# Attention and MLP on one core: a 128-wide left slice, normalisation in pieces, a fixed engine order

## The chip, the core and the metric

The kernel runs on one core of one Trainium2 chip. The metric is device time in microseconds (us) of one execution. The kernel before took 793.80, 796.29 and 796.85 us in three runs (median 796.29).

## What is computed

Eight batches, 12 heads, 448 tokens, head width 64. q and k are normalised per token and head, attention follows without a mask, the heads are joined to x of 768 columns, and a LayerNorm with an MLP of 3072 hidden columns is added to x. In numpy, cut:

```
q_n, k_n = rmsnorm(q, g_q), rmsnorm(k, g_k)
attn = softmax(q_n @ k_n.T / 8)
x = heads_joined(attn @ v)                # [8, 448, 768]
xn = (x - mean) / sqrt(var + 1e-6) * g_ln
out = x + relu(xn @ w_ch1) @ w_ch2
```

## The kernel before

Class `_Fast` does the work (lines 47 to 429). A last check on the softmax sums (`flag`, L408) would send the data through `_general`; the two are joined at L583 to L585.

**Attention** goes by head pairs: 6 pairs a batch, 48 in all. The 448 tokens of a head are 384, of which a partition holds three, and 64 left over; the left tokens of a pair's two heads share one group of 128 partitions. A unit is two pairs: `load_unit` (L89) brings q, k and v with three main loads and six for the leftovers on the SP queue, into one of two buffers. `prep_unit` (L102) normalises: Square on ScalarE (L108), sums on VectorE (L109), the root (`_rsqrt`, L31: a first guess by ScalarE's Exp from the exponent, then three Newton rounds on VectorE), k times g_q·g_k (L119) and times its root (L121), k as a high and a low half-precision part (L123, L124), q (L125, L127); v is cast on GpSimd (L129, L132). `trans_k` (L137) and `trans_q` (L151) turn seven groups each on TensorE, and VectorE copies the result to SBUF.

A pair has seven steps i. `scores(p, i)` (L164) multiplies 128 keys with 448 queries and ScalarE takes the exponential (L180); i = 6 has the leftover keys of both heads. `values(p - 1, i)` (L183) multiplies the pair before with v: three slices of 128 queries go to the accumulator oA (L202), the last 64 queries to oB (L204). A ones column in v gives the softmax sum, and `evac_o` (L208) divides by it.

**LayerNorm** (`ln`, L279 to L300) takes statistics of whole token tiles (three of 128 per batch, four in odd batches, whose fourth holds the leftovers of two batches), its root, and normalises on VectorE (L298). `ln_trans` (L302) turns it on TensorE. **The MLP** comes as chunks of six matmuls (`mlp_chunks`, L312): 24 `up` chunks (L323, Relu on ScalarE L325), then eight `down` chunks per tile (L334, added to x on VectorE L338, stored by SP, L353).

**The order.** `attention` (L226) is a generator; `run` (L359) draws steps from it with `upto`. It draws pair 0, then 12 loads of W1 between the next pairs (`load_w1`, L257: SP loads 256 columns into one of two staging buffers, GpSimd multiplies six times by g_ln, L264), then W2 by a casting load on GpSimd's queue (L268), then up to pair 7. After that, while batch b's MLP chunks are emitted, the steps of the next six pairs are drawn between them so that they are through at 0.78 of the chunks; then `ln` of the next batch, whose transposes go between the last chunks. The framework's scheduler orders each engine's instructions from this program; each engine and each DMA queue then runs its own in order.

Of the kernel before, what the change touches and what calls it, by code (L numbers as in the profile page):

```python
# [10 lines left out]
INT32 = mybir.dt.int32  # L11
# [6 lines left out]
LN2 = 0.6931471805599453  # L18
# [5 lines left out]
NU = 3  # L24
UH = H // NU
UG = UH * 3 + UH // 2
EXP_BIAS = -4.0
REC_LO, REC_HI = 1.0 / 3.0e7, 0.5


def _rsqrt(nc, eng, out, a, t0, t1, iters=3):  # L31
    eng.tensor_copy(out=t0, in_=a.bitcast(INT32))
    eng.tensor_scalar(out=t0, in0=t0, scalar1=2.0 ** -23, scalar2=-127.0,
                      op0=ALU.mult, op1=ALU.add)
    nc.scalar.activation(out, t0, AFT.Exp, scale=-0.5 * LN2)
    for _ in range(iters):
        eng.tensor_tensor(out=t1, in0=out, in1=out, op=ALU.mult)
        eng.tensor_tensor(out=t1, in0=t1, in1=a, op=ALU.mult)
        eng.tensor_scalar(out=t1, in0=t1, scalar1=-0.5, scalar2=1.5, op0=ALU.mult, op1=ALU.add)
        eng.tensor_tensor(out=out, in0=out, in1=t1, op=ALU.mult)  # L40
# [6 lines left out]
class _Fast:  # L47


    def __init__(self, ctx, tc, sh, q, k, v, w1, w2, out):  # L50
# [5 lines left out]
        self.p_t = pool("p_t", 1)  # L56
# [6 lines left out]
        self.p_st = pool("p_st", 2)  # L63
# [7 lines left out]
        self.v16 = [fix.tile([128, UH, 3, D + 1], FP16, name=f"v{i}", tag=f"v{i}") for i in range(3)]  # L71
        self.vl = [fix.tile([128, UH // 2, 2, D + 1], FP16, name=f"vl{i}", tag=f"vl{i}")
                   for i in range(3)]
        for t in self.kT:
            nc.vector.memset(t[:, 1], 0.0)
        for t in self.v16:
            nc.vector.memset(t[:, :, :, D], 1.0)
        for t in self.vl:
            nc.vector.memset(t, 0.0)
            nc.vector.memset(t[0:64, :, 0, D], 1.0)  # L80
            nc.vector.memset(t[64:128, :, 1, D], 1.0)
        self.rec = fix.tile([128, B * NPAIR, 3, 2], FP32, name="rec_all", tag="rec_all")
# [6 lines left out]
    def load_unit(self, u):  # L89
        nc = self.nc  # L90
        b, hs = u // NU, (u % NU) * UH
        t = self.p_in.tile([128, 3, UG, D], FP32, tag="qkv")
        for n, src in enumerate((self.q, self.k, self.v)):
            nc.sync.dma_start(
                t[:, n, 0:UH * 3].rearrange("p (h j) d -> p h (j d)", j=3),
                src[b, hs:hs + UH, 0:384].rearrange("h (p j) d -> p h (j d)", j=3))
            left = src[b, hs:hs + UH, 384:448].rearrange("(g e) p d -> e p g d", e=2)
# [4 lines left out]
    def prep_unit(self, u):  # L102
        nc, sh = self.nc, self.sh
        t = self.loads.pop(u)
        ssq = self.p_n.tile([128, 2, UG], FP32, tag="ssq")
        for n in range(2):
            sq = self.p_t.tile([128, UG, D], FP32, tag="sq", name="sq")
            nc.scalar.activation(sq, t[:, n], AFT.Square)  # L108
            nc.vector.tensor_reduce(out=ssq[:, n], in_=sq, axis=AX.X, op=ALU.add)  # L109
        msq = self.p_n.tile([128, 2, UG], FP32, tag="msq")  # L110
        nc.vector.tensor_scalar(out=msq, in0=ssq, scalar1=1.0 / D, scalar2=1e-6,
                                op0=ALU.mult, op1=ALU.add)
        rr = self.p_n.tile([128, 2, UG], FP32, tag="rr")
        t0 = self.p_n.tile([128, 2, UG], FP32, tag="rt0")
        t1 = self.p_n.tile([128, 2, UG], FP32, tag="rt1")
        _rsqrt(nc, nc.vector, rr, msq, t0, t1)
        qn = self.p_n.tile([128, UG, 2, D], FP16, tag="qn")
        khl = self.p_n.tile([128, UG, 2, D], FP16, tag="khl")
        nc.vector.tensor_tensor(out=t[:, 1], in0=t[:, 1],  # L119
                                in1=sh.gprod.unsqueeze(1).broadcast_to([128, UG, D]), op=ALU.mult)  # L120
        nc.vector.tensor_tensor(out=t[:, 1], in0=t[:, 1],  # L121
                                in1=rr[:, 1].unsqueeze(2).broadcast_to([128, UG, D]), op=ALU.mult)
        nc.vector.tensor_copy(out=khl[:, :, 0], in_=t[:, 1])  # L123
        nc.vector.tensor_tensor(out=khl[:, :, 1], in0=t[:, 1], in1=khl[:, :, 0], op=ALU.subtract)  # L124
        nc.vector.tensor_tensor(out=qn[:, :, 0], in0=t[:, 0],  # L125
                                in1=rr[:, 0].unsqueeze(2).broadcast_to([128, UG, D]), op=ALU.mult)
        nc.vector.tensor_copy(out=qn[:, :, 1], in_=qn[:, :, 0])  # L127
        v16, vl = self.v16[u % 3], self.vl[u % 3]
        nc.gpsimd.tensor_copy(out=v16[:, :, :, 0:D],  # L129
                              in_=t[:, 2, 0:UH * 3].rearrange("p (h j) d -> p h j d", j=3))  # L130
        for e in range(2):
            nc.gpsimd.tensor_copy(out=vl[64 * e:64 * e + 64, :, e, 0:D],  # L132
                                  in_=t[64 * e:64 * e + 64, 2, UH * 3:UG])
        self.units[u] = (qn, khl, v16, vl)


    def trans_k(self, p):  # L137
        nc, sh = self.nc, self.sh
        qn, khl, v16, vl = self.units[p // 2]
        w = p % 2  # L140
        ps = self.ps_tr.tile([128, 1024], FP16, tag="tr")
        kT = self.kT[p % 2]
        gs = [UH * 3 + w] + [6 * w + i for i in range(6)]
        for i, g in enumerate(gs):
            nc.tensor.matmul(ps[:, ts(i, 128)], khl[:, g], sh.id16, is_transpose=True,  # L145
                             start=(i == 0), stop=(i == 6))
        flat = kT.rearrange("p g d -> p (g d)")
        nc.vector.tensor_copy(out=flat[:, 0:64], in_=ps[:, 0:64])  # L148
        nc.vector.tensor_copy(out=flat[:, 128:960], in_=ps[:, 64:896])  # L149

    def trans_q(self, p):  # L151
        nc, sh = self.nc, self.sh
        qn, khl, v16, vl = self.units[p // 2]
        w = p % 2
        ps = self.ps_tr.tile([128, 1024], FP16, tag="tr")
        qT = self.p_qT.tile([128, 896], FP16, tag="qT")
        gs = [6 * w, 6 * w + 1, 6 * w + 2, UH * 3 + w, 6 * w + 3, 6 * w + 4, 6 * w + 5]
# [3 lines left out]
        nc.vector.tensor_copy(out=qT, in_=ps[:, 0:896])  # L161
        self.prs[p] = dict(qT=qT, kT=self.kT[p % 2])

    def scores(self, p, i):  # L164
# [6 lines left out]
        ps = self.ps_s.tile([128, 512], FP32, tag="psS")  # L171
# [11 lines left out]
    def values(self, p, i):  # L183
        nc = self.nc
        c = self.prs[p]
        qn, khl, v16, vl = self.units[p // 2]
        w = p % 2
        E = c["E"]
        if i == 0:
            c["oA"] = self.ps_o.tile([128, 3, 130], FP32, tag="oA", name="oA")  # L190
            c["oB"] = self.ps_o.tile([64, 130], FP32, tag="oB", name="oB")
        oA, oB = c["oA"], c["oB"]
        if i < 6:
            h, j = divmod(i, 3)
            rhs = v16[:, 2 * w + h, j]
            cs = slice(65 * h, 65 * h + 65)
            m0, l0 = (0, 384) if h == 0 else (64, 0)
        else:
            rhs = vl[:, w].rearrange("p e d -> p (e d)")
            cs, m0, l0 = slice(0, 130), 0, 384  # L200
        for t in range(3):
            nc.tensor.matmul(oA[:, t, cs], E[:, i, m0 + 128 * t:m0 + 128 * t + 128], rhs,  # L202
                             start=(i == 0 and t == 0), stop=(i == 6 and t == 2))
        nc.tensor.matmul(oB[:, cs], E[:, i, l0:l0 + 64], rhs, start=(i == 0), stop=(i == 6))  # L204
# [3 lines left out]
    def evac_o(self, p):  # L208
        nc = self.nc
# [5 lines left out]
        rec, recl = self.rec[:, p], self.recl[:, p]  # L215
        nc.vector.reciprocal(rec, oA[:, :, :, D])
        nc.vector.reciprocal(recl, oB[:, :, D])
        nc.vector.tensor_tensor(  # L218
            out=x[:, :, 128 * hp:128 * hp + 128].rearrange("p t (e d) -> p t e d", e=2),
            in0=oA[:, :, :, 0:D], in1=rec.unsqueeze(3).broadcast_to([128, 3, 2, D]), op=ALU.mult)  # L220
# [3 lines left out]
            in0=oB[:, :, 0:D], in1=recl.unsqueeze(2).broadcast_to([64, 2, D]), op=ALU.mult)  # L224

    def attention(self):  # L226

        n = B * NPAIR
        self.load_unit(0)
        self.load_unit(1)  # L230
        self.prep_unit(0)
        self.trans_k(0)
        self.trans_q(0)
        for p in range(n + 1):
# [5 lines left out]
            if p % 2 == 0 and p // 2 + 1 < B * NU:  # L240
                if p // 2 + 2 < B * NU:
                    self.load_unit(p // 2 + 2)
                self.prep_unit(p // 2 + 1)
            for i in range(7):
                if p < n:
                    self.scores(p, i)
                    yield p + (i + 0.5) / 7
                if p > 0:
                    self.values(p - 1, i)
                    yield p + (i + 1) / 7  # L250
                if p + 1 < n and i == 2:
                    self.trans_k(p + 1)
                if p + 1 < n and i == 4:
                    self.trans_q(p + 1)


    def load_w1(self, c0, c1):  # L257

        nc, sh = self.nc, self.sh
        st = self.p_st.tile([128, NDC, 256], FP32, tag="st", name="st")  # L260
        nc.sync.dma_start(st[:, :, 0:c1 - c0],
# [354 lines left out]
```

## Time and profile before

| | |
|---|---|
| median of three runs | 796.29 us |
| the profiled execution | 795.19 us, its span 793.4 us |
| TensorE (PE) busy | 697.7 us, 88% of the span, 5114 matmuls |
| VectorE (DVE) busy | 455.2 us, 57%, 1229 instructions |
| ScalarE (ACT) busy | 322.0 us, 41%, 609 instructions |
| GpSimd (POOL) busy | 119.8 us, 15%, 154 instructions |
| mean granted TensorE clock | 0.97 of 2.4 GHz |
| HBM read, written | 51.97 MB, 11.01 MB |

Times in the rows are microseconds from the span's start unless ns is said. PEld is TensorE's weight load, which overlaps PE. A row of the chain of waits gives start, duration and what it was, on the path that ended last. A group's row gives line, engine, operation, output and inputs with shapes, count, then busy time, mean ns of one, and idle time before them with what ended it. Matmuls are pipelined, so a busy TensorE need not be at its peak.

### The profile page before, as it was taken

The numbers are of one execution on the slowest core, as the hardware profiler recorded it, in microseconds if no ns is written. First come the engines' busy times: TensorE is split into PE (matmuls) and PEld (weight loads), VectorE is DVE, ScalarE is ACT, GpSimd is POOL, SyncE is SP. The second block draws the span as 40 slices with busy tenths as digits, with TensorE's granted clock in tenths as the row PEclk, the third lists the DMA queues.
The fourth block names the chain that finished last, engine by engine and source line by source line (L and its number), as shares of the span: only waits on it lengthen the run. The fifth ranks groups of instructions, "written<-read, shape, count | busy, mean of one in ns | idle before, by whom it ended". The sixth has DMA issues, their size and how long they took to land. (4 is left out here: it accounts for less than half of the span.)

```text
span 793.4 us, 12901 instructions
## 1 busy us (share of the span) xinstructions
PE 697.7 (88%) x5114; PEld 419.7 (53%) x5114; DVE 455.2 (57%) x1229; ACT 322.0 (41%) x609; POOL 119.8 (15%) x154
## 2 busy tenths in 40 slices
PE   0276438999999989999999999998999999999996
PEld 0144225655555656656555556655555666664453
DVE  2949369888546783678545683677545452334011
ACT  2163434743364316643464226642464216512400
POOL 2579992000000000010000000010000000000000
PEclk9997777999999999999999999999999999999999
DMA  8993642523021130233022130233020110001011
GB/s 195 239 259 124 190 131 70 140 71 110 21 71 46 61 95 21 70 91 91 21 71 64 47 97 14 70 91 90 21 70 1 40 41 1 2 21 41 0 41 43
DMA packets 76531, 59.17 MB, mean 75 GB/s; under 512 B 23728, under 2 KB 72880, under 8 KB 76464
## 3 DMA queue, kind: packets, MB, share of 16 engines
q1 hardware_dynamic: 72256, 53.49, 22.8%
q0 software_dynamic: 3136, 4.72, 3.3%
q8 instruction: 42, 0.69, 0.4%
q10 hardware_dynamic: 1072, 0.07, 0.1%
q14 instruction: 25, 0.20, 0.1%
HBM read 51.97 MB, written 11.01 MB: 79 GB/s over the span
## 5 line engine op out<-in xcount | busy, mean ns | idle before, releaser
L334 PE MATMUL psC<-w,hT 128*128 128x384 f16 x1344 | 245.8, 329 | 0.0
L323 PE MATMUL psH<-xnT,w 128*128 128x512 f16 (+1 forms) x1152 | 243.3, 353 | 1.8 <-DVE xnT L310 1.8
L180 ACT ACTIVATE E<-ps 128x448 f16<-128x448 f32 x336 | 178.3, 541 | 127.7 <-PE ps L174 100.5
L325 ACT ACTIVATE hT<-psH 128x384 f16<-128x384 f32 (+1 forms) x192 | 104.2, 543 | 162.6 <-PE psH L323 162.6
L334 PEld LDWEIGHTS <-hT 128*128 128x128 f16 x1344 | 125.8, 98 | 77.7 <-issue 1.9
L323 PEld LDWEIGHTS <-w 128*128 128x128 f16 x1152 | 106.5, 98 | 92.2 <-issue 2.6
L174 PE MATMUL ps<-qT,kT 128*128 128x448 f16 x288 | 105.7, 374 | 12.3 <-ACT E L180 7.6
L202 PEld LDWEIGHTS <-E 128*128 128x128 f16 x1008 | 72.7, 100 | 76.2 <-ACT E L180 16.9
L129 POOL CAST v<-t 128x768 f16<-128x768 f32 x24 | 22.0, 917 | 488.8 <-issue 430.5
L202 PE MATMUL oA<-v,E 128*128 128x65 f16 x864 | 74.5, 197 | 16.7 <-ACT E L180 10.4
L109 DVE TENSOR_REDUCE ssq<-sq 128x14 f32<-128x896 f32 x48 | 52.0, 1083 | 64.2 <-ACT sq L108 64.2
L108 ACT ACTIVATE sq<-t 128x896 f32<-128x896 f32 x48 | 45.5, 949 | 80.9 <-DMA t<-in_q_dram 66.0
L264 POOL TENSOR_SCALAR w<-st,gln 128x256 f16<-128x256 f32 x72 | 77.0, 1086 | 9.2 <-DMA st<-in_moe_w_ch_dram 8.9
L338 DVE TENSOR_TENSOR x<-psC,x 128x384 f32<-128x384 f32 x48 | 26.3, 548 | 80.9 <-PE psC L334 80.7
L145 PE MATMUL ps<-id,khl 128*128 128x128 f16 x336 | 29.9, 235 | 38.1 <-DVE khl L124 38.1
L204 PE MATMUL oB<-v,E 128*64 128x65 f16 x288 | 61.5, 219 | 0.4 <-DVE xl L222 0.4
L161 DVE COPY qT<-ps 128x896 f16<-128x896 f16 x48 | 29.7, 619 | 37.7 <-PE ps L159 37.5
L148 DVE COPY kT<-ps 128x64 f16<-128x64 f16 x48 | 9.0, 187 | 69.9 <-PE ps L145 69.7
L204 PEld LDWEIGHTS <-E 128*64 128x64 f16 x336 | 35.3, 107 | 25.3 <-issue 4.3
L145 PEld LDWEIGHTS <-khl 128*128 128x128 f16 x336 | 23.4, 106 | 44.7 <-DVE khl L124 38.4
L174 PEld LDWEIGHTS <-kT 128*128 128x128 f16 x288 | 27.9, 99 | 17.0 <-issue 5.3
L159 PE MATMUL ps<-id,qn 128*128 128x128 f16 x336 | 28.6, 228 | 5.1 <-DVE kT L149 4.9
(71 smaller groups left out, 549.7 us busy)
## 6 DMA issues: line engine op xcount, KB each, us to landing
t<-in_q_dram SPq DMA_DIRECT2D x24, 384.0 KB, 3.5
t<-in_k_dram SPq DMA_DIRECT2D x24, 384.0 KB, 4.3
t<-in_v_dram SPq DMA_DIRECT2D x24, 384.0 KB, 4.4
st<-in_moe_w_ch_dram SPq DMA_DIRECT2D x12, 768.0 KB, 5.1
out_dram<-x SPq DMA_DIRECT2D x24, 384.0 KB, 2.3
w<-in_moe_w_ch_dram POOLq DMA_DIRECT2D x4, 1152.0 KB, 13.4
t<-in_q_dram SPq DMA_DIRECT2D x48, 32.0 KB, 3.7
t<-in_k_dram SPq DMA_DIRECT2D x48, 32.0 KB, 3.8
```

The lines of the kernel that those rows point to most:

```text
L108: nc.scalar.activation(sq, t[:, n], AFT.Square)
L109: nc.vector.tensor_reduce(out=ssq[:, n], in_=sq, axis=AX.X, op=ALU.add)
L145: nc.tensor.matmul(ps[:, ts(i, 128)], khl[:, g], sh.id16, is_transpose=True, start=(i == 0), stop=(i == 6))
L161: nc.vector.tensor_copy(out=qT, in_=ps[:, 0:896])
L174: nc.tensor.matmul(ps[:, 0:S], kT[:, 192 + 128 * i:320 + 128 * i], qT[:, h * S:(h + 1) * S], start=True, stop=True)
L180: nc.scalar.activation(out=c["E"][:, i], in_=ps[:, 0:S], func=AFT.Exp, scale=1.0 / 8.0, bias=EXP_BIAS)
L202: nc.tensor.matmul(oA[:, t, cs], E[:, i, m0 + 128 * t:m0 + 128 * t + 128], rhs, start=(i == 0 and t == 0), stop=(i == 6 and t == 2))
L204: nc.tensor.matmul(oB[:, cs], E[:, i, l0:l0 + 64], rhs, start=(i == 0), stop=(i == 6))
L264: nc.gpsimd.tensor_scalar(out=sh.w1[:, dc, c0:c1], in0=st[:, dc, 0:c1 - c0], scalar1=sh.gln[:, dc:dc + 1], scalar2=None, op0=ALU.mult)
L323: nc.tensor.matmul(ps[:, 0:N], sh.w1[:, dc, ts(f, 128)], xnT[:, dc, 0:N], start=(dc == 0), stop=(dc == NDC - 1))
L325: nc.scalar.activation(out=hT[:, f, 0:N], in_=ps[:, 0:N], func=AFT.Relu)
L334: nc.tensor.matmul(ps[:, 0:384], hT[:, f, ts(t, 128)], sh.w2[:, f, ts(g, 384)], start=(f == 0), stop=(f == NFF - 1))
```

## The change

- The value matmul for the last 64 queries takes the 128 queries 320 to 447 as weights; rows 64 to 127 of its output are used. qT puts each head's 64 left queries last, so all slices start at multiples of 128, and the last score step has two matmuls of 448 columns in place of three.
- Units of batch 0 are one pair, and their buffers lie in hT, which the MLP uses later; units of the other batches stay two pairs. Their preparation is a list of 11 pieces, spread over the steps before the pair that needs them; a unit's loads are issued when the unit two ahead of it is prepared.
- k times g_q·g_k goes to GpSimd. The root has two rounds, and takes its guess from the integer bits in one Exp.
- W1 comes by three casting loads on GpSimd's queue, without g_ln; W2 by two.
- LN statistics are taken per pair (128 columns). LN's root, its passes (now ScalarE's Identity with scale and bias, then VectorE's product with g_ln) and its transposes are pieces between the last chunks, from 0.82 of a batch's MLP on.
- The first value matmuls of a pair are drawn one step later.
- TensorE, ScalarE, GpSimd and SP run in program order (`manual_schedule`); VectorE's order is still the scheduler's.

```diff
 def _rsqrt(nc, out, a, t, eps):
+    eng.tensor_scalar(out=a, in0=a, scalar1=eps, scalar2=None, op0=ALU.add)
+    nc.scalar.activation(out, a.bitcast(INT32), AFT.Exp, scale=-0.5 * LN2 * 2.0 ** -23,
+                         bias=0.5 * LN2 * (127.0 - 0.043))
+    for _ in range(2):
+        eng.tensor_tensor(out=t, in0=out, in1=out, op=ALU.mult)
+        eng.scalar_tensor_tensor(out=t, in0=t, scalar=-0.5, in1=a, op0=ALU.mult, op1=ALU.mult)
+        eng.scalar_tensor_tensor(out=out, in0=t, scalar=1.5, in1=out, op0=ALU.add, op1=ALU.mult)
...
 def load_unit(self, u):
+        if m == 1:
+            o = 2688 * (u % 3)
+            t = self.hT.rearrange("p f n -> p (f n)")[:, o:o + 2688].bitcast(FP32)
...
+        eng = nc.scalar if u < 2 else nc.sync
+        for n, src in ((1, self.k), (0, self.q), (2, self.v)):
...
-                nc.sync.dma_start(t[64 * e:64 * e + 64, n, UH * 3:UG], left[e])
+                eng.dma_start(t[64 * e:64 * e + 64, n, mh * 3:g], left[e])
...
 def prep_ops(self, u):
+        return [lambda: (begin(), square(1), kg()), lambda: total(1), lambda: square(0),
+                lambda: (total(0), vmain()), root, None, kn, khi, klo, qn, qdup, vleft]
...
 def scores(self, p, i):
-            nc.tensor.matmul(ps[:, 0:384], kT[:, 64:192], qT[:, 512:896], start=False, stop=False)
-            nc.tensor.matmul(ps[:, 384:448], kT[:, 64:192], qT[:, 448:512], start=False, stop=True)
+            nc.tensor.matmul(ps[:, 0:S], kT[:, 64:192], qT[:, S:2 * S], start=False, stop=True)
...
 def values(self, p, i):
-            c["oB"] = self.ps_o.tile([64, 130], FP32, tag="oB", name="oB")
+            c["oB"] = self.ps_o.tile([128, 130], FP32, tag="oB", name="oB")
...
-        nc.tensor.matmul(oB[:, cs], E[:, i, l0:l0 + 64], rhs, start=(i == 0), stop=(i == 6))
+        nc.tensor.matmul(oB[:, cs], E[:, i, 320:448], rhs, start=(i == 0), stop=(i == 6))
...
 def attention(self):
+        for u in range(1, nu):
+            p, m = UNIT_PAIR[u], UNITS[u][2]
+            st, e = max(7 * (p - 1 - m) + 2, last + 1), 7 * (p - 1) + 1
+            last = e
+            ops = self.prep_ops(u)
+            for x, op in enumerate(ops):
+                if op is not None:
+                    todo.setdefault(max(0, st + (e - st) * x // (len(ops) - 1)), []).append(op)
+            if u + 2 < nu and u + 2 > 2:
+                todo.setdefault(max(0, e), []).append(lambda u=u: self.load_unit(u + 2))
+        for u in range(3):
+            self.load_unit(u)
...
+                    for x in {0: (), 1: (0, 1)}.get(i, (i,)):
+                        self.values(p - 1, x)
+                if p > 1 and i == 1 and (p - 1) % NPAIR:
+                    self.stats(p - 2)
...
 def load_w1(self, c0, c1):
-        nc.sync.dma_start(st[:, :, 0:c1 - c0],
...
+        self.nc.gpsimd.dma_start(
+            out=self.sh.w1[:, :, c0:c1],
...
 def ln_ops(self, b):
+        def norm(t):
...
+            nc.scalar.activation(out=t32, in_=tiles[t], func=AFT.Identity,
+                                 scale=c["rs"][:, t:t + 1], bias=c["sh"][:, t:t + 1])
+            nc.vector.tensor_tensor(out=c["xn", t], in0=t32, in1=sh.gln, op=ALU.mult)
+
+        res = [root, lambda: norm(0)]
+        for t in range(1, n):
+            res += [lambda t=t: norm(t), lambda t=t: self.ln_trans(c["xn", t - 1], t - 1)]
+        return res + [lambda: self.ln_trans(c["xn", n - 1], n - 1)]
...
 def run(self):
+        upto(0.4)
+        for c in range(0, FF, 1024):
+            self.load_w1(c, c + 1024)
+        upto(3)
+        for n0 in range(0, NFF, 12):
+            self.load_w2(n0, n0 + 12)
         upto(7)
...
+        for op in self.ln_ops(0):
+            op()
+            upto(self.pos + 0.1)
+        frac = 0.82
...
+                upto(min(goal, start + (goal - start) * done / total / frac))
+                if self.pos >= goal:
+                    if items is None:
+                        items, at, left = self.ln_ops(b + 1), 0, len(chunks) - 1 - i
+                        per = len(items) / max(left - 1, 1)
+                        due = 0.0
+                    due += per
+                    while at < len(items) and at + 1 <= due + 1e-6:
+                        items[at]()
+                        at += 1
...
+        with tc.manual_schedule(engines={ENG.PE, ENG.Activation, ENG.Pool, ENG.SP}):
+            _Fast(fctx, tc, sh, q, k, v, moe_g_ln, moe_w_ch1, moe_w_ch2, out).run()
```

## Rows read from the trace of the kernel before

**Rows 1.** Stretches: us, busy of PE, PEld, DVE, ACT, POOL (count), clock, DMA, GB/s

```profile
0.00:131.40 131.40, 58.84 (x492) 37.41 (x493) 85.25 (x234) 46.56 (x85) 92.62 (x103) 0.86 0.71 182
131.40:205.00 73.60, 70.39 (x528) 43.69 (x528) 65.21 (x179) 35.45 (x71) 3.10 (x6) 1.00 0.30 87
```

**Rows 2.** One line, L323: ns min/median/max, first and last start, forms

```profile
L323 PE MATMUL psH<-xnT,w x1152: 322/358/390, 131.4 to 754.9; 128*128 128x384 f16 x96, 128*128 128x512 f16 x96
```

**Rows 3.** The chain of waits from 655 to 662 us

```profile
656.03 0.50 PE ps L159 x7
656.52 0.19 PE ps L174
656.71 0.09 PE oA L202 x3
656.80 0.15 PE oB L204
656.95 1.08 PE psH L323 x6
```

**Rows 4.** The chain of waits of the whole span

```profile
594.62 0.29 PE ps L174
...
648.20 0.97 PE psH L323 x6
```

**Rows 5.** Waits before 131.4 us: total, times, longest

```profile
ACT sq L108 <- DMA t<-in_q_dram: 32.8, 4, 10.4
```

**Rows 6.** Waits of SP's queue before 131.4 us

```profile
SPq L261 <- POOL w L264: 39.6, 7, 8.1
```

**Rows 7.** Timeline from 74 to 92 us, SP's queue and ScalarE

```profile
75.10 0.59 SPq L94 DMA_DIRECT2D t<-in_q_dram  x1
...
83.30 1.26 SPq L99 DMA_DIRECT2D t<-in_q_dram  x2
...
87.95 0.95 ACT L108 ACTIVATE sq<-t 128x896 f32<-128x896 f32 x1 [10.45 <-DMA t<-in_q_dram]
```

**Rows 8.** Timeline, ScalarE's first exponentials

```profile
34.17 0.98 ACT L180 ACTIVATE E<-ps 128x448 f16<-128x448 f32 x2 [8.54 <-PE ps L174]
```

**Rows 9.** Groups of TensorE from 131.4 us on

```profile
L204 PE MATMUL oB<-v,E 128*64 128x65 f16 x234 | 51.0, 218 | 0.0
```

**Rows 10.** Weight loads, by shape

```profile
L202 PEld LDWEIGHTS <-E 128*128 128x128 f16 x1008 | 72.7, 100 | 76.2 <-ACT E L180 16.9 <-issue 11.0 <-DVE x L218 7.2
...
L204 PEld LDWEIGHTS <-E 128*64 128x64 f16 x336 | 35.3, 107 | 25.3 <-issue 4.3 <-DVE xl L222 2.0
```

**Rows 11.** Groups of GpSimd, by shape

```profile
L264 POOL TENSOR_SCALAR w<-st,gln 128x256 f16<-128x256 f32 x72 | 77.0, 1086 | 9.2 <-DMA st<-in_moe_w_ch_dram 8.9
...
L129 POOL CAST v<-t 128x768 f16<-128x768 f32 x24 | 22.0, 917 | 488.8 <-issue 430.5 <-PE oB L204 32.9 <-DMA t<-in_v_dram 20.3
```

**Rows 12.** Groups of VectorE, by shape

```profile
L109 DVE TENSOR_REDUCE ssq<-sq 128x14 f32<-128x896 f32 x48 | 52.0, 1083 | 64.2 <-ACT sq L108 64.2
...
L121 DVE TENSOR_TENSOR t<-t,rr 128x896 f32<-128x896 f32 x24 | 26.3, 1097 | 0.5
...
L161 DVE COPY qT<-ps 128x896 f16<-128x896 f16 x48 | 29.7, 619 | 37.7 <-PE ps L159 37.5
...
L218 DVE TENSOR_TENSOR x<-oA,rec_all 128x384 f32<-128x384 f32 x48 | 26.2, 545 | 0.1
...
L222 DVE TENSOR_TENSOR xl<-oB,recl_all 64x128 f32<-64x128 f32 x48 | 13.4, 279 | 0.8
...
L292 DVE BATCH_NORM_STATS2 stat<-x 128x6 f32<-128x384 f32 x48 | 24.4, 539 | 0.2
...
L40 DVE TENSOR_TENSOR rr<-rr,t 128x28 f32<-128x28 f32 x72 | 14.9, 207 | 1.8
```

**Rows 13.** Waits of TensorE from 131.4 us on

```profile
PE psX L308 <- DVE xn L298: 6.5, 4, 2.0
...
PE oA L202 <- DVE x L218: 5.3, 10, 1.8
```

More of the change, by code (lines that the diff above doesn't have):

```diff
@@ L17 @@
 ts = bass.ts
-LN2 = 0.6931471805599453
 B, H, S, D = 8, 12, 448, 64
@@ L98, in load_unit, with prep_ops @@
             for e in range(2):
-                nc.sync.dma_start(t[64 * e:64 * e + 64, n, UH * 3:UG], left[e])
+                eng.dma_start(t[64 * e:64 * e + 64, n, mh * 3:g], left[e])
         self.loads[u] = t
-    def prep_unit(self, u):
+    def prep_ops(self, u):
         nc, sh = self.nc, self.sh
[L104 to L134, printed above, removed]
@@ new lines, in square, with total, root, kg @@
+        def square(n):
+            o = c["khl" if n == 1 else "qn"].rearrange("p g e d -> p (g e d)").bitcast(FP32)
+            c["sq", n] = o.rearrange("p (g d) -> p g d", d=D)
+            nc.scalar.activation(c["sq", n], c["t"][:, n], AFT.Square)
+        def total(n):
+            nc.vector.tensor_reduce(out=c["ssq"][:, n], in_=c["sq", n], axis=AX.X, op=ALU.add)
+        def root():
+            _rsqrt(nc, c["rr"], c["ssq"], c["rt"], D * 1e-6)
+        def kg():
+            nc.gpsimd.tensor_tensor(out=c["t"][:, 1], in0=c["t"][:, 1],
+                                    in1=sh.gprod.unsqueeze(1).broadcast_to([128, g, D]),
+                                    op=ALU.mult)
@@ L294, in ln @@
[L294 to L302 removed]
+        c = {}
@@ new lines, in ln_ops, with root @@
+        st = self.st[b]
+        mv = st[:, :, 6 * NPAIR:6 * NPAIR + 2]
+        def root():
+            c["rs"] = self.p_m.tile([128, 4], FP32, tag="rs", name="rs", bufs=2)
+            c["sh"] = self.p_m.tile([128, 4], FP32, tag="sh", name="sh", bufs=2)
+            for t in range(n):
+                nc.vector.bn_aggr(out=mv[:, t], in_=st[:, t, 0:6 * NPAIR])
+            _rsqrt(nc, c["rs"][:, 0:n], mv[:, 0:n, 1], st[:, 0:n, 0], 1e-6)
+            nc.vector.scalar_tensor_tensor(out=c["sh"][:, 0:n], in0=mv[:, 0:n, 0], scalar=-1.0,
+                                           in1=c["rs"][:, 0:n], op0=ALU.mult, op1=ALU.mult)
@@ L387, in run @@
             goal = NPAIR * (b + 2) + 1
-            done, xn, lt = 0.0, None, 0
+            done, items, at = 0.0, None, 0
             for i, (cost, emit) in enumerate(chunks):
@@ L391, in run @@
                 done += cost
-                f = done / total
-                if b + 1 < B:
-                    upto(min(goal, start + (goal - start) * f / frac))
-                    if xn is None and self.pos >= goal:
-                        xn, n = self.ln(b + 1)
-                    elif xn is not None and i >= len(chunks) - 1 - n and lt < n:
-                        self.ln_trans(xn, n, lt)
-                        lt += 1
+                if b + 1 == B:
+                    continue
+                upto(min(goal, start + (goal - start) * done / total / frac))
[8 more added lines that the diff above has]
+                        at += 1
             if b + 1 < B:
-                while lt < n:
-                    self.ln_trans(xn, n, lt)
-                    lt += 1
+                for op in items[at:]:
+                    op()
             if b + 2 == B:
```

273 lines of the change are left out of this document (133 added, 140 removed).

## The prediction, made before the changed kernel was run

> **What bounds the kernel now.** I read the stretches first, then the chain of waits, then matmul groups, waits and single durations. The stretch table [rows 1] splits the span at the first MLP matmul, which starts at 131.4 us [rows 2]. Before it TensorE is busy 58.8 of 131.4 us with a granted clock of 0.86; behind it 70.4 of 73.6 us at 1.00, the upper of its two levels (2.4 GHz). So there is a long start in which TensorE waits, and then TensorE is the bound for 655 us, and only work taken from its own stream or a hole in it counts there.
>
> Inside that stream the chain of waits [rows 3] gives each piece the time that it adds. Three value matmuls against full 128-query slices (oA) add 0.09 us, 0.03 each. The one against the last 64 queries (oB) adds 0.15, and whatever follows is late too: six MLP matmuls take 1.08 us behind an oB where they take 0.97 elsewhere [rows 4], and a score matmul 0.29 behind an oB [rows 4] where it takes 0.19 behind transposes [rows 3]. One 64-wide slice thus costs 0.12 + 0.10 = 0.22 us more than a 128-wide one.
>
> The start is a chain of late loads. ScalarE stands 32.8 us, in four waits of up to 10.4, before a Square whose q has not landed [rows 5]. The SP queue shows why: its W1 loads wait 39.6 us for the staging buffers that GpSimd multiplies [rows 6], and they stand ahead of the q, k, v loads. In one case q's main part is issued at 75.1, its leftover at 83.3, and the Square starts at 87.95 [rows 7]. ScalarE is in order, so the exponentials behind that Square stand too. The first exponential runs at 34.2 [rows 8].
>
> **The change, part by part.**
>
> *128-wide left slice.* By the first MLP matmul 9 of 48 head pairs are through their scores; of the rest, 234 oB records [rows 9] are 39 pairs x 6, and each pair has a seventh: 273 x 0.22 = 60 us off TensorE's stream. In the start the same saving is cover, TensorE waits there anyway. The lower bound is nothing (if the time hangs on something other than the width), the upper 64 us (0.235 each, the rounding of [rows 3, 4]). I take 60. The merging of two score matmuls into one leaves the columns as they are: nothing.
>
> By the Trainium skill (TensorE: Matmul & The Clock Gate, "LDWEIGHTS (loading the stationary operand)") a weight load takes the number of its columns / 1.2 ns, so the 64-wide slice should load in 53 ns, half of what the 128-wide one takes, and widening could only cost. By that rule the change would add up to 273 x 0.053 = 14 us to the stream (an estimate from that page). The trace disagrees: the 64-wide load takes 107 ns and the 128-wide one 100 [rows 10].
>
> *W1 by a casting DMA.* It removes 12 loads from SP's queue and 72 multiplications of 1.09 us from GpSimd [rows 11], and with them the four waits: 32.8 us. It puts three issues on GpSimd's queue, then two for W2; behind them stand v copies that are due a pair later. What is late next is VectorE. Its work for one single-pair unit, by [rows 12], with half of what an 896-wide instruction takes above a fixed 0.15 us (a little under the small ones' 0.2): two reductions 1.2, root of seven small ones 1.4, scaling k 0.6, cast 0.4, low part 0.6, q 0.65, copy 0.3 = 5.2 us; then kT copies 0.8, qT in three pieces 0.9, output scaling with two reciprocals 1.2, statistics 3 x 0.27 = 0.8: 8.9 us per pair.
>
> *Small units for batch 0.* The first unit's loads are half as large, but ScalarE now issues 12 leftover loads and three others before its first Square, at 0.63 each (two took 1.26 [rows 7]): first Square near 11 us. The chain for half the width (squares, reductions, root, scaling, 14 transposes, copies) is about 10 us: first scores at 21, 13 earlier than now. Bounds: no gain, and 18 us.
>
> *When the MLP starts.* By subtraction: 131.4 - 32.8 - 13 = 86 us. By VectorE: from 21 on, units 1 to 5 (about 23 us), unit 6 and 7 and part of 8 at 8 us each (19), copies for 8 pairs (14), seven output scalings (8.4), statistics (6) and the first normalisation (7) sum to 77, so 98 if nothing overlaps. I take 92, with 84 (the work packs better) and 115 (loads at the 182 GB/s of [rows 1] bound it) as the ends. Gain: 39 us. Eight pairs are done then against nine now, and a pair's own TensorE work is 14 transposes x 0.056, 8 scores x 0.19, 28 values x 0.03 = 3.2 us [rows 3]: 3 us back.
>
> *Statistics per pair, normalisation in pieces.* Between the last value matmul of a batch and its first LN transpose stands a chain: output scaling 1.2 us, 3 or 4 statistics of 0.27, as many aggregations of 0.19, root about 1.7, ScalarE's pass 0.95 (as the 896-wide Square of [rows 7], a little less), VectorE's product 0.95: 6.3 to 7 us. The order is now fixed: the arithmetic of the pieces puts the first transpose 3 chunks (2.9 us) behind the goal when the coming batch has four tiles and 5 chunks (4.9) when it has three. TensorE waits 4.1 us four times and 1.5 three times: 21 us, with the down chunks queued behind that transpose although they don't need it. Now its transposes wait 6.5 us for xn [rows 13], and with what the view doesn't list about 11 in all. So +10; bounds -6 (the pieces come in time) and +20.
>
> *k times gains on GpSimd.* It takes a 1.08 us pass off VectorE, 24 times, off TensorE's path. No row has a two-input product on GpSimd: the cast of 768 columns at 0.92 us gives 1.07 for 896, the scaling of 256 at 1.09 gives 3.8 [rows 11]. I take 2, nearer to the cast, which has the same number of columns. It is issued six steps, some 8 us, ahead of its reader; without that cover at most 27 x 3.8 us would show.
>
> *The rest.* The shorter root saves VectorE 8 small instructions of 0.2 per unit [rows 12]; smaller copies and statistics give about as much back. In the saturated stretch VectorE is busy 65 of 74 us [rows 1], so this is cover, with little left over. The output accumulator's wait, 5.3 us now [rows 13], gets a step more of slack but a tighter VectorE: nothing. LN's pass on ScalarE, 28 x 0.95, lies in the down phases, where ScalarE has no Relu. The tail is unchanged.
>
> **Sum.** The profiled execution took 795.2 us (span 793.4); the median of three is 796.3. 795.2 - 60 - 39 + 3 + 10 = 709, at the median 710.
>
> **Rivals.**
> - *The start is better packed, transposes don't wait:* MLP at 84 and LN at +2: 710 - 8 - 8 = 694, and to 680 if both ends are reached. For it: VectorE instructions overlap at their ends. Against it: the LN chain is longer than three chunks.
> - *Loads bound the start:* units, W1 and W2 are all wanted in the first 110 us. MLP at 115: 733. For it: 182 GB/s in the start now [rows 1]. Against it: W1 is wanted in thirds.
> - *Fixed order shows VectorE's queue:* ScalarE's root waits for VectorE's reductions with exponentials behind it, and TensorE's next score behind those. If each of 40 pairs loses 1 us: 750. For it: VectorE's 65 of 74 us. Against it: preparation starts 13 steps ahead.
> - *The change doesn't do what it says:* if what oB costs comes from the turn to another accumulator and not from its width, 60 us stay: 770. Against it: transposes turn to another accumulator too, and a score behind them takes 0.19 [rows 3]. The page's rule on weight loads would make it 784.
> - *Slower than before:* SP's order is now fixed as well, and a store waiting for its chunk stands ahead of a unit's loads. If they land too late, ScalarE's Square stalls everything, as in the start now, 8.2 us each time. For 21 two-pair units the new kernel is slower once the mean stall passes (796 - 710) / 21 = 4.1 us; at 8.2 us it takes 882. Against it: a load is issued 15 steps (some 24 us) ahead of its Square, and the leftover of [rows 7] had landed 4.65 us after its issue.
>
> By the Trainium skill (GPSIMD Engine Reference, "4.1 Engine selection") two-input elementwise work belongs on VectorE, GpSimd being about twice as slow. That gives about 2 us per unit (an estimate), which no run here shows yet and which the six steps cover.
>
> **How the numbers follow.** Forecast 0.60, with a range of its own of 694 to 728; better packed 0.12; loads 0.13; VectorE's queue 0.08; no effect of the width 0.04, of which 0.01 for the page's rule; slower 0.03. The range 680 to 745 takes in the forecast, nearly all of the better case and the loads, and a third of VectorE's queue: 8 in 10. A measurement of this kernel tells 0.5% (4 us) from no change. All cases but the last lie more than that below 796: faster 0.96, the same 0.01, slower 0.03.
>
> **What would show it.** The chain of waits should have oB at 0.03 and the score behind it at 0.19; if oB still adds 0.15, the first step is wrong. The first MLP matmul should start near 92 us, the first exponential near 22, with no Square waiting for q over 2 us. The first LN transpose of a batch should wait 1 to 4 us for xn. VectorE should be the busiest engine of the start. A TensorE stream with holes under the value or score matmuls in every pair would make the forecast wrong, towards 750.

## The result, and the profile after

The changed kernel takes 734.1 us (median of 4 runs, 733.0 to 734.9), beside it the kernel before 795.0 (791.4 to 796.9): ratio 0.924, 95% interval 0.920 to 0.928. The forecast was 710, so the change is faster by 61 us where 86 were forecast. 734 lies in the range, and it is the time of the rival "Loads bound the start" (733), though only half of the late start turns out to be that rival's. The profiled execution took 733.0 us, its span 731.2.

The first MLP matmul is where I split the span again. Groups of TensorE, then stretches (us, busy of PE, PEld, DVE, ACT, POOL with counts, clock, DMA share, GB/s), of the kernel after:

```profile
L394 PE MATMUL psH<-xnT,w x1152: 323/352/390, 117.5 to 693.1; 128*128 128x384 f16 x96, 128*128 128x512 f16 x96
```

```profile
0.00:20.00 20.00, 0.00 (x0) 0.00 (x0) 4.90 (x18) 3.47 (x6) 3.82 (x12) 1.00 0.44 126
20.00:40.00 20.00, 10.93 (x70) 6.54 (x71) 16.86 (x51) 7.80 (x19) 7.94 (x14) 1.00 0.59 126
40.00:60.00 20.00, 10.68 (x114) 7.28 (x112) 17.08 (x53) 9.19 (x21) 6.17 (x10) 0.91 1.13 219
60.00:80.00 20.00, 4.40 (x42) 2.88 (x41) 9.75 (x27) 5.66 (x12) 2.38 (x2) 0.64 1.15 219
80.00:117.50 37.50, 21.00 (x186) 13.89 (x184) 31.01 (x85) 17.50 (x32) 8.67 (x11) 0.69 0.67 155
117.50:731.20 613.70, 586.32 (x4662) 356.75 (x4661) 348.36 (x968) 294.62 (x560) 60.69 (x72) 0.98 0.19 57
```

The MLP starts at 117.5 us, not at 92 [rows 2: 131.4 before]. From there to the end it takes 613.7 us; the forecast had 662.0 - 60 + 3 + 10 = 615. That the two agree within 1.3 us is in part luck (below), but the whole miss lies in the start. There, from 40 to 80 us, the DMA moves 219 GB/s without a break while TensorE is busy 4.4 us of the second 20.

The saturated stream is as the first step had it. The chain of waits of the kernel after, 300 to 302 us:

```profile
300.34 0.19 PE psS L217
300.53 0.09 PE oA L241 x3
300.62 0.03 PE oB L243
300.65 0.97 PE psH L394 x6
301.62 0.19 PE psS L220
```

oB adds 0.03 and six MLP matmuls behind it 0.97, where [rows 3] had 0.15 and 1.08.

In the start the waits show late loads, but not those of before. Waits before 117.5 us (total, times, longest), kernel after:

```profile
PE psK L186 <- DVE khl L156: 20.0, 3, 13.8
...
ACT khl L136 <- DMA t<-in_k_dram: 10.5, 2, 6.4
```

And the timelines of GpSimd and of SP's queue, which show who was ahead of whom:

```profile
29.98 1.14 POOL L145 TENSOR_TENSOR hT<-hT,gprod 128x448 f32<-128x448 f32 x1 [9.07 <-issue]
31.06 2.66 POOL L315 DMA_DIRECT2D w<-in_moe_w_ch_dram  x3
...
45.70 2.10 POOL L320 DMA_DIRECT2D w<-in_moe_w_ch_dram  x2
```

```profile
52.31 0.41 SPq L106 DMA_DIRECT2D t<-in_q_dram  x1
53.25 5.92 SPq L111 DMA_DIRECT2D t<-in_q_dram  x2
...
59.86 7.80 SPq L111 DMA_DIRECT2D t<-in_v_dram  x2
...
95.78 1.24 SPq L111 DMA_DIRECT2D t<-in_v_dram  x2
```

W1 is issued at 31.1, W2 at 45.7. Pairs of leftover loads hold SP's queue for 5.9 and 7.8 us while the weights are under way, and for 1.24 at 96 us; ScalarE's Square waits up to 6.4 us for its k, and TensorE 13.8 us in one piece for what VectorE makes of it.

Behind 117.5 us TensorE has one kind of wait left that adds up to more than 1.2 us. Its row, from there on, in the kernel after (in [rows 13] it was 6.5 us):

```profile
PE psX L379 <- DVE xn L366: 19.7, 7, 4.4
```

### The profile page after: what moved, and what is told of

It is laid out like the page before. It is cut to its first block, busy times and chain, and to the rows that moved or that the text cites. A ratio compares the mean times of both kernels' runs of the same rounds, so it can differ in the third digit from the quotient of the medians.

```text
span 731.2 us, 12852 instructions
## 1 busy us (share of the span) xinstructions
PE 633.3 (87%) x5066; PEld 387.3 (53%) x5066; DVE 428.0 (59%) x1195; ACT 338.2 (46%) x646; POOL 89.7 (12%) x119
## 4 chain that ended last, share of the span: by engine, by line
PE 74%; DVE 11%; DMA 6%; SPq 3%; ACT 3%; issue 1%; ACTq 0%; DVEq 0%
PE psH L394 30%; PE psC L405 25%; PE psS L217 6%; PE oA L241 4%; SPq L111 3%; PE psQ L200 2%; DMA t<-in_k_dram 2%; PE psK L186 2%; DMA hT<-in_q_dram 2%; PE psX L379 2%; PE oB L243 1%; DMA hT<-in_v_dram 1%; ACT t L364 1%; DVE xn L366 1%; DVE x L258 1%
## 5 line engine op out<-in xcount | busy, mean ns | idle before, releaser
L222 ACT ACTIVATE E<-psS 128x448 f16<-128x448 f32 x336 | 179.1, 540 | 119.9 <-PE psS L217 99.1
L217 PE MATMUL psS<-qT,kT 128*128 128x448 f16 x288 | 105.3, 373 | 8.0 <-ACT E L222 5.2
L241 PEld LDWEIGHTS <-E 128*128 128x128 f16 x1008 | 74.4, 101 | 68.5 <-issue 20.8
L145 POOL TENSOR_TENSOR t<-t,gprod 128x896 f32<-128x896 f32 x21 | 43.7, 2081 | 455.0 <-issue 271.7
L186 PE MATMUL psK<-id,khl 128*128 128x128 f16 x336 | 29.2, 232 | 43.6 <-DVE rt L39 23.6
L243 PE MATMUL oB<-v,E 128*128 128x65 f16 x288 | 53.5, 197 | 0.3
L139 DVE TENSOR_REDUCE ssq<-khl 128x14 f32<-128x896 f32 (+1 forms) x27 | 26.4, 979 | 26.3 <-ACT khl L136 25.8
L202 DVE COPY qT<-psQ 128x448 f16<-128x448 f16 x48 | 18.7, 389 | 38.6 <-PE psQ L200 38.6
L339 DVE BATCH_NORM_STATS2 stat<-x 128x6 f32<-128x128 f32 x144 | 34.5, 282 | 0.7
L243 PEld LDWEIGHTS <-E 128*128 128x128 f16 x336 | 33.3, 99 | 1.4 <-DVE xl L263 0.9
L200 PE MATMUL psQ<-id,qn 128*128 128x128 f16 x336 | 29.2, 232 | 4.9 <-DVE kT L190 4.9
```

What stands on the lines that cost most here:

```text
L145: nc.gpsimd.tensor_tensor(out=c["t"][:, 1], in0=c["t"][:, 1], in1=sh.gprod.unsqueeze(1).broadcast_to([128, g, D]), op=ALU.mult)
L200: nc.tensor.matmul(ps[:, ts(i, 128)], qn[:, g], sh.id16, is_transpose=True, start=(i == 0), stop=(i == 6))
L217: nc.tensor.matmul(ps[:, 0:S], kT[:, 192 + 128 * i:320 + 128 * i], qT[:, h * S:(h + 1) * S], start=True, stop=True)
L222: nc.scalar.activation(out=c["E"][:, i], in_=ps[:, 0:S], func=AFT.Exp, scale=1.0 / 8.0, bias=EXP_BIAS)
L241: nc.tensor.matmul(oA[:, t, cs], E[:, i, ts(t, 128)], rhs, start=(i == 0 and t == 0), stop=(i == 6 and t == 2))
L243: nc.tensor.matmul(oB[:, cs], E[:, i, 320:448], rhs, start=(i == 0), stop=(i == 6))
```

## The experiments

Times are medians of 4 runs (two without the fixed order), or of the one run that the row names. "MLP" is the start of the first MLP matmul, "rest" the span behind it. The kernel before, run beside them, took 795.0 to 799.4 us in the median, so a difference of 1 or 2 us between rows says little.

| run | time, us | ratio to before (95%) | MLP | rest |
|---|---|---|---|---|
| after | 734.1 | 0.924 (0.920 to 0.928) | 117.5 | 613.7 |
| W2 late | 722.8 | 0.906 (0.901 to 0.911) | 105.8 | 615.0 |
| W1 and W2 late | 721.0 | one run | 104.6 | 614.6 |
| left slice 64 wide again | 796.5 | one run | 120.6 | 674.1 |
| before, slice 128 wide | 765.4 | one run | 126.9 | 636.7 |
| no step of delay | 752.8 | 0.942 (0.939 to 0.945) | 119.2 | 633.2 |
| LN transposes late | 709.3 | 0.892 (0.888 to 0.896) | 119.1 | 587.2 |
| k times gains on VectorE | 733.3 | 0.922 (0.918 to 0.926) | 117.6 | 613.6 |
| no fixed order | 740.5 | 0.930 (0.924 to 0.936) | 123.8 | 617.1 |
| W2 and LN late | 695.9 | 0.875 (0.871 to 0.879) | 105.9 | 587.1 |
| and unit 1's leftovers on SP | 692.0 | 0.869 (0.864 to 0.873) | 103.5 | 588.6 |
| and kT by ScalarE | 696.0 | 0.874 (0.869 to 0.878) | 108.3 | 586.3 |
| W2 and LN late, k times gains on VectorE | 696.7 | 0.875 (0.870 to 0.879) | 106.3 | 588.4 |

**The loads of the start.** The first run issues W2 only when the attention of batch 0 is drawn, the second W1 too:

```diff
-        upto(3)
+        upto(7)
         for n0 in range(0, NFF, 12):
             self.load_w2(n0, n0 + 12)
-        upto(7)
```

> W2's two casting loads are issued behind step 7 instead of behind step 3. Theory A (the weights crowd the q, k, v loads out of the DMA engines, which moved 217 to 221 GB/s from 40 to 90 us): 9.4 MB, some 43 us of transfers, leave that stretch, Squares wait under 8 us in all for their loads instead of 18, and the first MLP matmul moves from 117.5 to about 100; time 715 to 722, if W2 still lands before the first down chunk. Theory B (the fixed order and VectorE's work set the pace of the start): the first MLP matmul stays at 113 to 118, time 730 to 736.

> Both weights are loaded only behind step 7, to see the start's pace without them. Theory A: no Square waits more than 2 us for its load, pair 6's last exponential runs at 80 to 88 us instead of about 105, and the MLP then waits for W1; the time itself says little (720 to 745). Theory B: pair 6's last exponential stays near 105.

Stretches of the run with W2 late, then of the run with both late:

```profile
40.00:60.00 20.00, 12.64 (x108) 8.45 (x107) 16.44 (x55) 9.79 (x21) 4.21 (x8) 0.69 1.13 219
60.00:80.00 20.00, 10.45 (x89) 6.97 (x87) 18.44 (x49) 9.54 (x18) 9.23 (x8) 0.67 0.64 162
```

```profile
40.00:60.00 20.00, 13.29 (x120) 8.81 (x118) 17.41 (x62) 10.44 (x25) 4.77 (x8) 0.76 0.63 171
60.00:80.00 20.00, 9.06 (x81) 6.09 (x79) 19.31 (x43) 8.24 (x15) 10.32 (x9) 0.67 0.09 23
```

With W2 out of the way VectorE works 18.4 of the 20 us from 60 to 80 instead of 9.8, and the MLP starts 11.7 us earlier (100 was expected). Taking W1 away too empties the DMA of that stretch (23 GB/s); the last scores of pair 6 then run at 88.1 us instead of 101.1, no Square behind the first waits for a load, and the MLP starts 1.2 us earlier still, in one run. So W2 is what crowds the unit loads out, worth some 11 us of time, and the other 12.6 us of the start's lateness (104.6 against 92) are not the weights. The expectation put W2 at 43 us of transfers from its 9.4 MB in HBM. The GB/s of the rows count what is written: two transfers of 2304 KB, 4.7 MB, so some 22 us at 219 GB/s.

**The width.** One run puts the 64-wide slice back into the changed kernel, the other puts the 128-wide slice alone into the kernel before (the copies of q reordered and the two score matmuls merged as in the change):

```diff
-        nc.tensor.matmul(oB[:, cs], E[:, i, 320:448], rhs, start=(i == 0), stop=(i == 6))
+        nc.tensor.matmul(oB[64:128, cs], E[:, i, 384:448], rhs, start=(i == 0), stop=(i == 6))
```

> The changed kernel with the left slice narrowed to 64 queries again (its output in rows 64 to 127), all else kept. If the width is what oB cost: 40 pairs x 7 x 0.22 = 62 us come back in the saturated part, time 790 to 798, and a score matmul behind an oB takes 0.29 in the chain of waits. If not: 734 to 740.

```diff
-        oB = self.ps_o.tile([64, 130], FP32, tag="oB", name="oB")
+        oB = self.ps_o.tile([128, 130], FP32, tag="oB", name="oB")
...
-                nc.tensor.matmul(oB[:, cs], E[:, i, l0:l0 + 64], rhs,
+                nc.tensor.matmul(oB[:, cs], E[:, i, 320:448], rhs,
```

> The kernel before with the 128-wide left slice alone (and the qT layout and score matmuls that go with it). If the width is what oB cost: 39 pairs x 7 x 0.22 = 60 us less than before, time 733 to 740. If not: 790 to 800.

The chain of the changed kernel with the 64-wide slice:

```profile
301.16 0.19 PE psS L217
301.35 0.09 PE oA L241 x3
301.44 0.15 PE oB L243
301.58 1.08 PE psH L394 x6
302.66 0.19 PE psS L220
```

The 0.15 and the 1.08 of [rows 3] are back, and the rest grows by 674.1 - 613.7 = 60.4 us, 0.22 for each of 40 pairs x 7. By the Trainium skill (TensorE: Matmul & The Clock Gate, "LDWEIGHTS (loading the stationary operand)") the narrower load should be the cheaper one; this pair of runs says the opposite, by 60 us.

In the kernel before the same width takes only 662.0 - 636.7 = 25 us off the rest, and 34 off the time (799.4 beside it, one run), where 60 were expected. TensorE's busy time of the rest falls by 50 us (638.8 to 588.5), but its idle time grows by 25 (23.2 to 48.2). Waits of TensorE there from 126.9 us on, then VectorE's share of the MLP's first stretch:

```profile
PE oA L202 <- DVE x L218: 16.6, 15, 2.5
PE ps L159 <- DVE kT L149: 8.1, 6, 2.0
```

```profile
126.90:200.50 73.60, 63.62 (x512) 39.83 (x511) 64.33 (x185) 35.84 (x71) 3.97 (x6) 0.98 0.31 87
```

TensorE waits for VectorE's output scaling now (5.3 us before [rows 13], 16.6 here), with VectorE busy 64.3 of 73.6 us. The changed kernel has no such waits; the product of k and the gains on GpSimd isn't why (below). One candidate is that the first value matmuls of a pair come a step later. The run takes that back in the changed kernel:

```diff
-                    for x in {0: (), 1: (0, 1)}.get(i, (i,)):
+                    for x in (i,):
```

> The changed kernel with the first value matmuls of a pair back in the step with its next pair's first scores, as before the change: the accumulators are wanted one step earlier. In the kernel before with a 128-wide slice alone the value matmuls waited 16.6 us for VectorE's output scaling behind the first MLP matmul. Theory (the step of delay is what covers that scaling): such waits come back, 10 to 20 us, and the time is 744 to 755. Rival (VectorE, busy two thirds of the MLP stretch here and not seven eighths as there, is early enough without the step): waits under 5 us, 732 to 739.

The rest grows by 19.5 us. Waits of TensorE from 119 us on in that run:

```profile
PE oA L241 <- DVE x L258: 8.2, 12, 1.3
PE oB L243 <- DVE xl L263: 2.2, 14, 0.2
```

The waits are back, 10.4 us in the rows named (the weight loads ahead of these matmuls wait 21.3 us, for 2.9 in the changed kernel), and TensorE's busy time grows by 8.8 us (586.3 to 595.1). The step of delay, which I had costed at nothing, is worth 19 us: without it a third of what the width saves is lost. The other 16 us between 25 and 60 weren't traced to one part of the change; that VectorE has 37 us less to do in the rest (348.4 us for 385.2) is a candidate.

**The LN transposes.** The coming batch's LN begins at a goal reached earlier (0.76 of the chunks for 0.82), with the root and the passes of two tiles at the goal, and the transposes come one per chunk at the end; the run changes the two together:

```diff
-        frac = 0.82
+        frac = 0.76
...
-                    due += per
-                    while at < len(items) and at + 1 <= due + 1e-6:
-                        items[at]()
-                        at += 1
+                    elif i >= len(chunks) - 1 - nt and at < len(items):
+                        for op in items[at]:
+                            op()
+                        at += 1
```

> The changed kernel with the LN of the coming batch placed otherwise: root and the first tiles' passes at the goal, which is reached earlier (0.76 of the chunks instead of 0.82), and the transposes one per chunk at the end, so that each has 3 or more chunks for its chain. Theory (TensorE waits about 4.7 us before four of the LN transposes and 0.8 before three, because they are issued 3 or 5 chunks behind the goal): these waits fall from 21 us to 5 or less, and the time from 734 to 717 to 722. Rival (the wait only moves, because attention is drawn faster and VectorE falls behind): waits on x, kT or E take its place and the time stays within 4 us of 734.

It brings 24.8 us, more than the 12 to 17 expected and more than the 20 us of waits. The rest shrinks by 26.5 us (613.7 to 587.2): TensorE's idle time by 17.7, as some 2 us of small waits come new, and its busy time by 8.8 (586.3 to 577.5). The busy time is the clock. TensorE's timeline of the kernel after around one such wait, and two stretches of it:

```profile
338.85 0.82 PE L379 MATMUL psX<-id,xn 128*128 128x128 f16 x6 [4.44 <-DVE xn L366]
339.46 3.40 PE L405 MATMUL psC<-w,hT 128*128 128x384 f16 x12
...
343.03 2.11 PE L405 MATMUL psC<-w,hT 128*128 128x384 f16 x12
```

```profile
338.00:343.60 5.60, 4.75 (x28) 2.95 (x29) 3.83 (x6) 2.66 (x3) 0.00 (x0) 0.70 0.00 0
343.60:348.00 4.40, 4.40 (x36) 2.84 (x35) 2.40 (x5) 0.00 (x0) 0.00 (x0) 1.00 0.00 0
```

Behind the 4.44 us hole twelve down matmuls take 3.40 us, a little later the same twelve 2.11, and the granted clock is 0.70 in that stretch and 1.00 behind it: so part of it ran at the lower of the two levels (1.2 GHz). That is 1.3 us there and 0.3 on the transposes (0.82 against 0.50), 1.6 us. Behind the other three long waits, at 180, 497 and 653 us, the same matmuls lose 2.6, 2.9 and 1.6 us (at 180 and 497 the twelve take 4.05), 8.7 in all. Behind the three short waits, of 0.66 us, they lose nothing: the clock is 1.00 around the one at 267 us. With the transposes late, no wait for xn is listed behind 119 us and the clock of the rest is 1.00:

```profile
119.10:706.30 587.20, 577.52 (x4662) 353.72 (x4661) 348.54 (x968) 293.12 (x560) 60.80 (x72) 1.00 0.21 60
```

**The product of k and gains, and the fixed order.** One run has `nc.vector` for `nc.gpsimd` in `kg`, the other leaves out `manual_schedule`.

> The changed kernel with the product of k and the gains on VectorE again, at 1.08 us a two-pair unit there instead of 2.08 on GpSimd. Theory (VectorE bounds the start, and has room later): 8 pairs of the start cost about 0.6 us each, 5 us in all, less what VectorE's subtraction loses when it falls on the GpSimd product (2.15 instead of 0.6 us in some units of the start); the rest of the span stays: 734 to 740. Rival (the GpSimd product holds up VectorE's subtraction everywhere, and is what makes the start late): 720 to 730.

> The changed kernel without the fixed order: the scheduler orders all engines. Theory (the fixed order costs the 21 us before the LN transposes, and nothing else hangs on it): 710 to 725, with the LN waits gone. Rival (the fixed order is what keeps VectorE's and GpSimd's work in time for TensorE): waits under scores and values appear, 740 to 770.

Neither side of the first was right: nothing moves (733.3 us for 734.1). VectorE is busy 83.0 us before the MLP instead of 79.6, and has room for it beside its waits for loads. The product on GpSimd takes 2.08 us, and nobody waits for it. Group of the kernel after:

```profile
L145 POOL TENSOR_TENSOR t<-t,gprod 128x896 f32<-128x896 f32 x21 | 43.7, 2081 | 455.0 <-issue 271.7
```

The free order costs 6.4 us. At 740.5 (742.8 and 738.2) it touches the rival's range, but the waits under scores and values that the rival named are not there beyond 0.4 us. Waits of TensorE behind 123.8 us in it:

```profile
PE psX L379 <- DVE xn L366: 11.7, 9, 2.5
PE psQ L200 <- DVE kT L190: 9.6, 10, 1.6
```

In the scheduler's order TensorE waits less for xn (11.7 for 19.7), but q's transposes wait for the copies of kT; the rest is 3.4 us longer, and the MLP starts 6.3 us later. So the fixed order as a whole is no loss; the place that it gives the LN transposes is one.

**Together, and what is left of the start.** One run joins W2 late and LN late, and three build on it, the second of them on the run with unit 1's loads on SP as well:

> The later W2 of the first experiment (722.8) and the later LN transposes of the fifth together. Theory (the two losses lie in different stretches, the start and the ends of the MLP batches, and add): 722.8 less 12 to 17, so 706 to 711. Rival (a common limit, VectorE, takes back part): 712 to 720.

> The kernel with late W2 and late LN transposes, and the six leftover loads of unit 1 issued by SP instead of ScalarE. Theory (ScalarE's own DMA issues hold its first Square until 15.8 us, and the rest of the start follows from it): first Square near 12, first MLP matmul near 102 instead of 105.9, 690 to 693. Rival (VectorE's work of unit 1 comes later by as much, so the start doesn't move): 695 to 698.

```diff
-        eng = nc.scalar if u < 2 else nc.sync
+        eng = nc.scalar if u < 1 else nc.sync
```

> The same as the run before it, and in the first 8 pairs ScalarE instead of VectorE copies the transposed k out of PSUM (0.19 and 0.58 us a pair on VectorE, 6 us in all). Theory (once the loads are out of the way VectorE bounds the start, busy 79.7 of the first 105.9 us and over 8.2 of every 10 from 20 us on): the first MLP matmul 4 to 6 us earlier than in that run, the time too. Rival (the chain of one unit, not the sum of VectorE's work, sets the pace): no change within 2 us, or ScalarE's order puts exponentials behind the copies and 2 to 5 us are lost.

```diff
+        if p < 8:
+            nc.scalar.activation(out=flat[:, 0:64], in_=ps[:, 0:64], func=AFT.Identity)
+            nc.scalar.activation(out=flat[:, 128:960], in_=ps[:, 64:896], func=AFT.Identity)
+        else:
```

> Late W2, late LN transposes, and the product of k and the gains on VectorE. In the start it adds 6 x 0.61 + 2 x 1.08 = 5.8 us to VectorE and takes away what VectorE's subtraction loses on meeting the GpSimd product (about 4 us by its rows). Theory (VectorE's sum bounds the start now): first MLP matmul 1 to 6 us later than 105.9, the time 697 to 702; in the MLP stretch no change. Rival (the subtraction's collision is what counts): 690 to 695.

The two add: 734.1 - 11.3 - 24.8 = 698.0, and 695.9 is measured, less than was expected because the LN's share was larger. Handing unit 1's leftover loads to SP brings 3.9 us more, to 692.0, the fastest of all; the MLP starts 2.4 us earlier. The chain of the first unit shows why. ScalarE's timeline in the kernel after, and then in that run:

```profile
2.19 4.48 ACTq L111 DMA_DIRECT2D hT<-in_k_dram  x2
...
13.21 1.21 ACTq L111 DMA_DIRECT2D hT<-in_v_dram  x2
14.46 1.28 ACT L136 ACT_TABLE_LOAD   x1 [14.46 <-DMA hT<-in_q_dram]
15.75 0.58 ACT L136 ACTIVATE khl<-hT 128x448 f32<-128x448 f32 x1
...
28.40 0.98 ACT L222 ACTIVATE E<-psS 128x448 f16<-128x448 f32 x2 [7.39 <-PE psS L217]
```

```profile
11.26 1.28 ACT L136 ACT_TABLE_LOAD   x1 [11.26 <-DMA hT<-in_q_dram]
12.56 0.58 ACT L136 ACTIVATE khl<-hT 128x448 f32<-128x448 f32 x1
...
25.12 0.98 ACT L222 ACTIVATE E<-psS 128x448 f16<-128x448 f32 x2 [7.30 <-PE psS L217]
```

The Square comes 3.2 us sooner and the first exponential 3.3; from one to the other it is 12.6 us in both. Beside W2 and LN late, which differs by this edit alone and has them at 16.9 and 29.5 us, it is 4.4 us for each.

Taking 6 us of copies off VectorE moved the MLP back from 103.5 to 108.3 us. VectorE's busy time up to the MLP fell from 81.2 to 77.0, but ScalarE, which issues in order, now stood before the copies (waits of that run before 104 us):

```profile
ACT kT L190 <- PE psK L186: 15.7, 7, 4.8
```

Its Squares came later for it, and VectorE, which from 20 us to the MLP had waited 7.9 us in all and for no Square, now waited 16.8, 11.0 of them for Squares. So this run doesn't show what less work for VectorE alone would bring.

With the product on VectorE in place of GpSimd (W2 and LN late) the MLP starts 0.4 us later and the time is 696.7, 0.8 more: the move to GpSimd is worth next to nothing here too. Part of VectorE's gain goes elsewhere: its two subtractions for khl that are 896 wide take 1860 ns in the mean in the first 106 us with the product on GpSimd, one 2.64 us and one 1.08, and 1088 with it on VectorE. The groups in this order:

```profile
L156 DVE TENSOR_TENSOR khl<-t,khl 128x896 f16<-128x896 f32 x2 | 3.7, 1860 | 0.0
```

```profile
L156 DVE TENSOR_TENSOR khl<-t,khl 128x896 f16<-128x896 f32 x2 | 2.2, 1088 | 0.0
```

## Why the prediction was right, and where it was not

**128-wide slice, 60 us: right**, 60.4 on the chip in the stretch it was counted in. The rival "the change doesn't do what it says" is out: with all else of the change in place, the narrow slice alone costs it. But "the output accumulator's wait ... nothing" hid a condition: with the width alone, half is given back to waits for VectorE. The step of delay, which I costed at nothing as "a step more of slack", carries 19 us. Why a narrow slice costs more than a wide one is open: the runs show what it adds, not where in TensorE.

**When the MLP starts, 92: wrong by 25.5 us, and this is the whole miss.** The failing step is *W1 by a casting DMA*, in the sentence "What is late next is VectorE". What is late next is the unit loads, because of W2. I moved five large transfers onto a queue with nothing to hold them and counted their issues, not their bytes. In the kernel before, W2's four loads are issued at 1.3, 18.7, 23.0 and 45.1 us; in the changed one its two wait for the program's order, are issued at 45.7, behind W1, and are under way when the units of the next batch want their loads. W2 isn't wanted before the first down matmul, and costs some 11 us there. (Issuing it early, as before, wasn't tried.) I had the case as a rival with 115 us and 733, and argued against it that "W1 is wanted in thirds"; W1 is indeed nearly harmless (1 us, one run). That the rival's 733 was met is partly luck, since the weights make up 12.9 of the 25.5 us (117.5 to 104.6).

Of the other 12.6 us, 8.7 lie before the first exponential and 3.9 behind it. With both weights late it runs at 29.7 us, where scores were forecast at 21, and the MLP starts 74.9 us later, where 92 - 21 = 71 was taken. VectorE's sum for that stretch was 77 (by its own price of 5.2 units 1 to 5 make 26 us, not 23, so 80), and the 6 us that I took off for overlap hardly came: it is 76.4 us with W2 and LN late, and 78.4 with unit 1's loads on SP. VectorE's waits speak for it as the one that sets the pace once W2 is out of the way: with both weights late they are 6.5 us from 20 us to the MLP, with 76.0 of 84.6 us busy; in the changed kernel they are 20.3. So VectorE was the right engine, one step too early. That is read from its waits; no run lightens VectorE alone.

**Small units, first scores at 21: too early.** The first Square is at 15.75 instead of 11, because a pair of leftover loads takes ScalarE 1.2 to 4.5 us where I took 0.63 each, and because of the table load of 1.28 us ahead of the Square, which I left out. From there to the first exponential it is 12.6 us instead of 10, with VectorE at work on unit 1 in between. Of the 6 us by which the first exponential misses 22 (28.4), the MLP gets back 2.4 when unit 1's loads go to SP.

**LN, +10: right in the waits, short in their price.** Forecast 4.1 us four times and 1.5 three times, 21 in all; it was 4.4 four times and 0.66 three times, 19.7. The term for the clock was missing: 1.6 to 2.9 us behind each of the four long ones, 8.7 in all. Without the waits the rest takes 26.5 us less, so the place of the LN pieces cost more than it was charged, and it is the change's one fault found behind the start. That the rest still came out within 1.3 us of the sum is partly luck: the wait for output scaling, 5.3 us in [rows 13], went down to 0.2, which the sum had at nothing, and works against the clock.

**kg on GpSimd, 2 us, hidden: right** (2.08 us, no change of the time). By the Trainium skill (SBUF — State Buffer, "SBUF: two separate sides") a VectorE instruction with two inputs in SBUF and a GpSimd instruction that reads SBUF share a pair of ports; whichever starts first holds it to its end, and the other waits. The subtraction above agrees: the one of 2.64 us begins 0.64 us behind a GpSimd product and ends 0.95 us behind that product's end. In that start it gives back some 1.5 of the 5.8 us that the move saves.

**VectorE's queue, 750: didn't come.** No wait of TensorE under scores or values behind 117.5 us adds up to more than 0.2 us.

## What to carry to other kernels

When large loads change their queue or their place in the order, count their bytes and not only their issues: add them up against what else wants the DMA in that stretch, and keep what is wanted later out of it. Price a hole in a saturated TensorE stream by the hole and by the slower clock behind it. And a saving on the busiest engine counts only as far as the next one keeps up: look for the slack that the same change gives, or try the saving alone.

## What the runs showed of the hardware

- A 64-column slice of weights between 128-column ones cost 0.22 us more than another 128-column one (60.4 us over 40 x 7 of them): its load takes no less time than theirs (107 and 100 ns [rows 10]), and the six matmuls behind it take 1.08 us instead of 0.97.
- A hole of 4.44 us in a stream at 2.4 GHz was followed by work at a lower clock (a mean of 0.70 over 5.6 us), in which twelve 128x384 matmuls took 3.40 us instead of 2.11; four such holes cost 8.7 us beside their own length. A hole of 0.66 us was followed by none (1.00).
- With casting DMAs under way (219 GB/s from 40 to 80 us) the issue of a pair of leftover loads held SP's queue for up to 7.8 us, against 1.24 later: the queue is held at the issue, not only at the landing. With both weights late such pairs took 1.1 to 2.3 us from 39 to 57 us (170 GB/s), and 4.4 and 4.6 us at 82 and 90, when the weights were under way.
- A VectorE subtraction of two inputs that began 0.64 us behind a GpSimd product took 2.64 us instead of 1.08 (W2 and LN late).
